# A linear attention feeding two gated layers on one core: another program order of the opening, and a subtraction moved from GpSimd to VectorE inside the weight decoding

## The chip, the core and the metric

The kernel runs on one NeuronCore of a Trainium2 chip. Its engines run side by side, each through its own queue in order: TensorE (PE, matrix products; PEld are its weight loads), VectorE (DVE), ScalarE (ACT), GpSimd (POOL), and SyncE (SP), which here issues every DMA. The metric is the device time of one execution in microseconds, lower is better.

## The reference

```
# r,k,v: (4 batches, 8 heads, 768 tokens, 48)
for t in range(S):
    cur = (u*k_t) outer v_t
    y_t = r_t @ (state + cur)
    state = w*state + k_t outer v_t
x  = y as (3072 tokens, 384)
h  = x @ w_in                                # 384 -> 2048
x  = (h * clip(h+3, 0, 6) / 6) @ w_out       # 2048 -> 384
out = (sigmoid(x @ w_gate) * (x @ w_val)) @ w_out2   # 384 -> 1536 -> 384
```

All inputs and the output are float32.

## The kernel before

**Attention.** 24 chunks of 128 tokens (chunk c is batch c mod 4, sequence part c div 4). `load_chunk` fetches a chunk twice: `rk` (r and k transposed, 448 KB) and `vkr` (natural order, 576 KB). `prep` scales them on VectorE, or on GpSimd for r·k and k from chunk 8 on, and makes on ScalarE the eight diagonal tiles of `aeo`. `stage_A` forms k·r products on TensorE, which VectorE then copies under a mask into `aeo` (L297, L298). `stage_Y` computes y, ScalarE copies it to `ysb` (L355, L358), and four DMAs per chunk lay it out as `xf`, features by tokens. `stage_U` updates the state `Z`. `split_chunk` turns `xf` into a rounded part `xhi` (ScalarE, L370) and the rest `xlo` (VectorE, L371), so that three fast products give a float32 one.

**Weights.** 34 pairs of weight tiles come as 64-bit words (`raw`, 768 KB each). Decoding a pair is a pipeline of three slots (`slot`): ScalarE reads the words (L78, L79), VectorE joins them in four operations (L85, L87, L89, L91), then ScalarE makes the rounded half (L135) and VectorE the rest (`w`, L123). A call of `slot` does one of these steps for each of three pairs. `fetch_next` issues the loads.

**Feed-forward.** Stage one works on six blocks of 512 tokens (four chunks each), each in 16 steps f: nine products `h`, then on ScalarE t (L559), on VectorE t (L560), `gh` on ScalarE (L393) and `gl`, the rest t - gh, on VectorE or GpSimd (L394). Two steps later nine products `o` follow (`out1`). `steps1` is the order of the steps: the first LEAD steps of block 0 alone, then block 1 and block 0 in turn. Step numbers i count in that order. The products of a step's first half of tokens (`halves`) are issued ahead for i = 0 and 1. A psum buffer of `h` is one of two, so the products of step i wait for t of step i-2. Stage two has six blocks of 12 steps: nine products `h` (gate), nine `pv`, sigmoid, t (L646), `gh`, `gl` on GpSimd, and twelve products `o` two steps later.

**What sets the order.** Up to step i = LEAD+2 a scheduler places the instructions of each engine from the program's order and its own estimate of times; from i = LEAD+3 on the program's order holds (`manual_schedule`). `due` gives the steps at which the attention stages of later blocks run. The last block of stage one calls `slot` in every odd step, stage two in every step while pairs are left. At the end, `values_load` brings a flag into a register of every engine, and a branch skips a fallback loop.

**Buffers that matter here.** `wpool` has 17 buffers for `raw`, `w` and, for the first four chunks, `vkr` and `aeo`. `ysb` has one buffer, `xf` three, `rk` three.

Of the kernel before, what the change touches and what calls it, by code (L numbers as in the profile page):

```python
# [63 lines left out]
def decay_attention_ffn_ffn(ctx, tc, rkT, vkr, wT, uN, uT, flip_d, ident_d, mask_d, wst, out):  # L64
# [13 lines left out]
        nc.scalar.activation(a.bitcast(F32), raw[:, :, 1].bitcast(F32), AF.Abs)  # L78
        nc.scalar.activation(r, raw[:, :, 0], AF.Copy, scale=2.0 ** -29)  # L79

    def join_words(*tiles):

        for a, r, raw in tiles:
            af = a.bitcast(F32)
            nc.vector.tensor_scalar(out=af, in0=af, scalar1=TOP, scalar2=BOTTOM, op0=ALU.min, op1=ALU.max)  # L85
        for a, r, raw in tiles:
            nc.vector.tensor_scalar(out=a, in0=a, scalar1=3, scalar2=0x3FFFFFF8, op0=ALU.logical_shift_left, op1=ALU.bitwise_and)  # L87
        for a, r, raw in tiles:
            nc.vector.scalar_tensor_tensor(out=a, in0=raw[:, :, 1], scalar=0xC0000000, in1=a, op0=ALU.bitwise_and, op1=ALU.bitwise_or)  # L89
        for a, r, raw in tiles:  # L90
            nc.vector.tensor_tensor(out=a, in0=a, in1=r, op=ALU.add)  # L91
# [32 lines left out]
        for x, (kind, f) in enumerate(PAIRS[i]):  # L124
            parts[kind][f] = w[:, :, x * DM:(x + 1) * DM]

    def slot(early=None, n_early=0):

        old, mid = pipe
        new = None  # L130
        if old:
            i, a, raw = old
            pool = early if NP1 <= i < NP1 + n_early else wpool
            w = pool.tile([P, 2, 2 * DM], F32R, tag="w", name="w")
            nc.scalar.activation(w[:, 0, :], a.bitcast(F32), AF.Copy)  # L135
        if count["begun"] < count["fetched"]:
            k = count["begun"]
            raw = raws.pop(k)
            b = dec_p.tile([P, 2 * DM], U32, tag="a", name="a")
            read_words(b, raw[:, :, 0], raw)  # L140
            new = k, b, raw
            count["begun"] += 1
        if mid:
            join_words((mid[1], mid[2][:, :, 0], mid[2]))
        if old:
            finish((i, a, w))
        pipe[:] = mid, new
# [109 lines left out]
    def prep(c, part):  # L257

        if c >= n_chunks:
            return  # L260
        if part == 0:
            t, n = loads.pop(c)
            v, k, r = n[:, 0], n[:, 1], n[:, 2]
            for p in ((0, 2), (2, 4)) if c == 0 else ((0, 4),):
                tp = t[:, :, p[0]:p[1]]
                nc.vector.tensor_tensor(out=tp, in0=tp, in1=wb[:, :, p[0]:p[1]], op=ALU.mult)
            side = nc.vector if c < 2 * B else nc.gpsimd
            side.tensor_tensor(out=r, in0=r, in1=k, op=ALU.mult)  # L268
            side.tensor_tensor(out=r, in0=r, in1=uB, op=ALU.mult)
            prepped[c] = {"R": t[:, 0], "K": t[:, 1], "v": v, "k": k, "r": r}  # L270
            return
        q = prepped[c]
        if part == 1:
            q["c"] = a2.tile([C, H], F32, tag="cd", name="cd")
            nc.vector.tensor_reduce(out=q["c"], in_=q["r"], axis=mybir.AxisListType.X, op=ALU.add)  # L275
        elif part == 2:
            pool, tag = (wpool, "w") if c < B else (a2, "aeo")
            ab = pool.tile([C, 2, NP, C], F32, tag=tag, name="aeo")
            for i, nm in enumerate(("ae", "ao")):
                q[nm] = ab[:, i]  # L280
                cs = q["c"].rearrange("p (n x) -> p n x", x=2)[:, :, i:i + 1]
                for p in range(NP):
                    nc.scalar.activation(q[nm][:, p, :], flip, AF.Copy, scale=cs[:, p, :])  # L283
        elif c // B < NCH - 1:
            side = nc.vector if c < 2 * B else nc.gpsimd
            side.tensor_tensor(out=q["k"], in0=q["k"], in1=WN, op=ALU.mult)
# [41 lines left out]
    def stage_Y(c):  # L328
        q = prepped[c]
        n, b = c // B, c % B  # L330
        pool, tag = (ps_o, "o") if c < B else (ps_h, "h") if c in BETWEEN else (ps_a, "A")
        ps = [pool.tile([P, NP, C], F32, tag=tag, name="y") for _ in range(1 if n == 0 else 2)]

        def place(x, p):

            y = p % 2
            m = D if y else 64
            return ps[x if n > 0 else 0][64 * y:64 * y + m, 2 * x + p // 2, :], m

# [12 lines left out]
        def after():
            ysb = a1.tile([ROWS, NP, C], F32, tag="ysb", name="ysb")
            if n == 0:
                nc.scalar.activation(ysb, ps[0][0:ROWS], AF.Copy)  # L355
            else:
                for x in range(2):
                    nc.scalar.activation(ysb[:, 2 * x:2 * x + 2, :], ps[x][0:ROWS, 2 * x:2 * x + 2, :], AF.Copy)  # L358
            x = xf[c] = xf_p.tile([P, KC, C], F32, tag="xf", name="xf")
            for kc, (r0, nr, q0) in ((0, (0, 32, 0)), (1, (32, 16, 0)), (1, (64, 16, 16)), (2, (80, 32, 0))):  # L360
                nc.sync.dma_start(out=x[4 * q0:4 * (q0 + nr), kc, :], in_=ysb[r0:r0 + nr])
        return after
# [25 lines left out]
        return ps  # L388

    def split_g(g, n, side):  # L390
        gh = g_p.tile([P, 512], F32R, tag="gh", name="gh")
        gl = g_p.tile([P, 512], F32R, tag="gl", name="gl")
        nc.scalar.activation(gh[:, :n], g[:, :n], AF.Copy)  # L393
        side.tensor_tensor(out=gl[:, :n], in0=g[:, :n], in1=gh[:, :n].bitcast(F32), op=ALU.subtract)  # L394
        return gh, gl

    three = const.tile([P, 1], F32, name="three")
# [1 line left out]

    LEAD = 6
    steps1 = [(0, f) for f in range(LEAD)]
    for f in range(F1):
        steps1 += [(1, f)] + [(0, f + LEAD)] * (f + LEAD < F1)
# [34 lines left out]
    due = []  # L440
    for j in range(1, len(BLOCKS1)):
        these = [x for x in stages if x[2] == j]
        first, span = (1, LEAD - 1) if j == 1 else (LEAD + 2, 2 * F1 - 2 - LEAD - 2) if j == 2 else (F1 * (j - 1), F1)
        due += [first + span * k // len(these) for k in range(len(these))]

    nxt = 0
# [10 lines left out]
    load_chunk(1)  # L457
    load_chunk(2)
    load_chunk(3)
    fetch1(4)  # L460
    powers()
    on_a, on_y = {}, {}
    for c in range(B):
        for part in range(3):
            prep(c, part)
        on_a[c] = stage_A(c)
        if c == 0:
            wtab = powers_ahead()
        if c == 1:
            power_transposes(wtab)  # L470
        if c > 0:
            on_a[c - 1]()
            on_y[c - 1] = stage_Y(c - 1)
            slot()
        if c > 1:
            on_y[c - 2]()
            fetch1(3 + c)
    on_a[B - 1]()
    on_y[B - 1] = stage_Y(B - 1)
    slot()  # L480
# [15 lines left out]
    split_chunk(3)  # L496
    slot()
    prep(3, 3)
    load_chunk(B)
    fetch1(6)  # L500
    load_chunk(B + 1)

    st1 = starts(BLOCKS1)
    outs = {}
# [46 lines left out]
    last = F1 * (len(BLOCKS1) - 1)  # L551
    pending = []
    for i, (j, f) in enumerate(steps1):
        if i == LEAD + 3:
            ctx.enter_context(tc.manual_schedule())
        n = BLOCKS1[j]
        ps = proj_into(halves[i], win[f], xs[j], n, HALF) if i < 2 else proj(win[f], xs[j], n)
        t = t_p.tile([P, 512], F32, tag="t", name="t")
        nc.scalar.activation(t[:, :n], ps[:, :n], AF.Relu, bias=three)  # L559
        nc.vector.scalar_tensor_tensor(out=t[:, :n], in0=t[:, :n], scalar=6.0, in1=ps[:, :n], op0=ALU.min, op1=ALU.mult)  # L560
        gs[i] = split_g(t, n, nc.vector if i < 2 * F1 else nc.gpsimd)
        pending.append(i)
        if i == 0:
            after_u = stage_U(2)
# [39 lines left out]
            fetch_next(3, w2pool)  # L604
        if i >= last:
            next_x1(0, f)
            if f % 2 == 1:
                slot(w2pool, EARLY)
                fetch_next(1, w2pool)


    steps2 = [(j, f) for j in range(len(BLOCKS2)) for f in range(F2)]
# [25 lines left out]
    for i, (j, f) in enumerate(steps2):  # L638
        n = BLOCKS2[j]
        x = xs[("2", j)]  # L640
        pg = proj(wga[f], x, n)
        pv = ps_a.tile([P, 512], F32, tag="A", name="pv")
        proj_into(pv, wva[f], x, n)
        t = t_p.tile([P, 512], F32, tag="t", name="t")
        nc.scalar.activation(t[:, :n], pg[:, :n], AF.Sigmoid)  # L645
        nc.vector.tensor_tensor(out=t[:, :n], in0=t[:, :n], in1=pv[:, :n], op=ALU.mult)  # L646
        gs[i] = split_g(t, n, nc.gpsimd)
        if f >= LAG:
            out2(i - LAG)
        slot(w2pool, EARLY)  # L650
        fetch_next(1, w2pool)
        if j + 1 < len(BLOCKS2):
            next_x1(j + 1, f)
        if f == F2 - 1:
            for k in range(LAG):
                out2(i - LAG + 1 + k)
# [2 lines left out]


    T = 32
    bad = nc.values_load(outside, min_val=0, max_val=1)
    with tc.If(bad > 0):
        x0 = tc.dram_tile([DM, NT], F32, name="x0")
        with ExitStack() as fb:
# [168 lines left out]
```

## Time and profile before

| | |
|---|---|
| median of 3 runs | 1000.77 us (999.6 to 1002.5) |
| the profiled execution | 1000.27 us, its span 998.5 us |
| PE busy | 953.9 us, 96% |
| PEld busy | 800.0 us, 80% |
| DVE busy | 437.4 us, 44% |
| ACT busy | 397.6 us, 40% |
| POOL busy | 240.2 us, 24% |
| mean granted clock of TensorE | 0.981 of 2.4 GHz |

A profile is one execution. Busy shares are means over stages with different limits, so the tables by stretch below say more. The DMA share is the mean over 16 DMA engines. Of the 24 chunks' attention, the loads and the decoding, most lies beside the products; what is outside them is at the start, at the change from stage one to stage two, and at the end.

### The profile page before, as it was taken

To read this page: it belongs to the slowest core of one execution; us is meant where nothing else is said; L and a number is where in the kernel's file an instruction comes from. 1 tells how busy PE (TensorE), PEld (TensorE's weight loads), DVE (VectorE), ACT (ScalarE), POOL (GpSimd) and SP (SyncE) were. 2 spreads that over 40 slices of the span, in tenths; PEclk is the share of its full clock that TensorE was granted. 3 is DMA by queue.
4 is the path that set the end of the run, shared out by engine and by line. 5 is a ranking of instruction groups with operands and counts; after the bars stand their busy time and mean duration, and the time that the engine had idled before them with its cause. 6 is when DMAs were issued, how large, how long until landed. Compare 5 with 4: busy or idle time off the path is not lost.

```text
span 998.5 us, 13269 instructions
## 1 busy us (share of the span) xinstructions
PE 953.9 (96%) x5320; PEld 800.0 (80%) x5320; DVE 437.4 (44%) x645; ACT 397.6 (40%) x754; POOL 240.2 (24%) x188
## 2 busy tenths in 40 slices
PE   5589799999999999999999999999999999999997
PEld 4477587788888888787887887888888888888886
DVE  7999587544344434323576995122122122122111
ACT  3857274444444444443556663222222222222211
POOL 0003201103444543432332221221221221221221
PEclk9679999999999999999999999999999999999999
DMA  9754241131312222100612441001001001000001
GB/s 304 216 195 164 77 142 30 52 106 43 90 52 82 63 89 82 51 17 23 238 64 71 168 142 43 22 1 55 9 1 55 9 1 56 9 1 32 1 1 35
DMA packets 38582, 72.10 MB, mean 72 GB/s; under 512 B 4208, under 2 KB 26096, under 8 KB 38512
## 3 DMA queue, kind: packets, MB, share of 16 engines
q1 hardware_dynamic: 38512, 71.17, 22.7%
q8 instruction: 43, 0.70, 0.3%
q14 instruction: 27, 0.22, 0.1%
HBM read 57.00 MB, written 9.44 MB: 67 GB/s over the span
## 4 chain that ended last, share of the span: by engine, by line
PE 83%; DMA 5%; DVE 5%; ACT 2%; issue 2%; POOL 1%; SPq 0%; POOLq 0%; ACTq 0%; DVEq 0%
PE o L110 32%; PE h L110 31%; PE pv L110 15%; DMA vkr<-in_vkr 3%; PE y L110 3%; PE A L110 2%; DMA xf<-ysb 1%; POOL gl L394 1%; DVE w L123 1%; DVE t L560 1%; ACT aeo L283 1%; PE U L110 1%; DVE a L91 1%; DVE a L89 1%; ACT gh L393 1%
## 5 line engine op out<-in xcount | busy, mean ns | idle before, releaser
L110 PE MATMUL h<-xhi,w 128*128 128x512 f32 (+1 forms) x1020 | 343.6, 393 | 4.3 <-DVE t L560 2.8
L394 POOL TENSOR_TENSOR gl<-t,gh 128x512 fp32r<-128x512 f32 x136 | 178.5, 1312 | 567.0 <-ACT gh L393 561.4
L110 PEld LDWEIGHTS h<-xhi,w 128*128 128x128 f32 x1020 | 193.1, 190 | 46.0 <-DVE t L560 4.0
L393 ACT ACTIVATE gh<-t 128x512 fp32r<-128x512 f32 x168 | 106.1, 632 | 238.9 <-DVE t L646 156.0
L110 PE MATMUL h<-xlo,w 128*128 128x512 f32 (+1 forms) x510 | 199.8, 392 | 1.4 <-DVE xlo L371 1.3
L110 PE MATMUL o<-gh,w 128*128 128x512 f32 x576 | 195.0, 396 | 0.0
L646 DVE TENSOR_TENSOR t<-t,pv 128x512 f32<-128x512 f32 x72 | 49.5, 687 | 267.8 <-PE pv L110 266.9
L110 PE MATMUL o<-w,gh 128*128 128x384 f32 x576 | 147.5, 336 | 1.1 <-DVE w L123 1.0
L110 PE MATMUL pv<-xhi,w 128*128 128x512 f32 x432 | 144.8, 389 | 1.1 <-DVE w L123 1.1
L560 DVE SCALAR_TENSOR_TENSOR t<-t,h 128x512 f32<-128x512 f32 x96 | 65.7, 686 | 179.8 <-ACT t L559 179.8
L110 PEld LDWEIGHTS o<-gh,w 128*128 128x128 f32 x576 | 108.4, 188 | 24.9 <-issue 0.9
L559 ACT ACTIVATE t<-h,three 128x512 f32<-128x512 f32 x96 | 65.5, 685 | 132.5 <-PE h L110 130.7
L110 PE MATMUL o<-gl,w 128*128 128x512 f32 x288 | 113.5, 394 | 3.2 <-DVE gl L394 2.4
L110 PEld LDWEIGHTS h<-xlo,w 128*128 128x128 f32 x510 | 96.8, 190 | 19.6 <-DVE xlo L371 1.9
L110 PEld LDWEIGHTS o<-w,gh 128*128 128x128 f32 x576 | 105.6, 188 | 6.4 <-DVE w L123 1.3
L110 PE MATMUL o<-w,gl 128*128 128x384 f32 x288 | 97.0, 337 | 0.0
L110 PEld LDWEIGHTS pv<-xhi,w 128*128 128x128 f32 x432 | 81.1, 188 | 18.6 <-DVE w L123 1.5
L645 ACT ACTIVATE t<-h 128x512 f32<-128x512 f32 x72 | 42.9, 596 | 131.3 <-PE h L110 131.2
L110 PE MATMUL pv<-xlo,w 128*128 128x512 f32 x216 | 84.0, 389 | 0.0
L268 POOL TENSOR_TENSOR vkr<-vkr 128x384 f32<-128x384 f32 x16 | 30.1, 1882 | 179.4 <-DMA vkr<-in_vkr 179.4
L110 PEld LDWEIGHTS o<-gl,w 128*128 128x128 f32 x288 | 54.5, 189 | 14.7 <-DVE gl L394 2.8
L283 ACT ACTIVATE aeo<-flip,cd 128x128 f32<-128x128 f32 x192 | 58.7, 392 | 6.6 <-DVE cd L275 6.6
(68 smaller groups left out, 805.5 us busy)
## 6 DMA issues: line engine op xcount, KB each, us to landing
raw<-in_weights SPq DMA_DIRECT2D x34, 768.0 KB, 5.7
vkr<-in_vkr SPq DMA_DIRECT2D x24, 576.0 KB, 5.0
rk<-in_rkT SPq DMA_DIRECT2D x24, 448.0 KB, 4.3
x<-ob SPq DMA_DIRECT2D x18, 256.0 KB, 2.1
x2f<-x SPq DMA_DIRECT2D x24, 192.0 KB, 3.0
out<-ob SPq DMA_DIRECT2D x24, 192.0 KB, 1.9
xf<-ysb SPq DMA_DIRECT2D x48, 64.0 KB, 2.1
xf<-ysb SPq DMA_DIRECT2D x48, 32.0 KB, 2.0
```

Source lines behind the costliest of these rows:

```text
L89: nc.vector.scalar_tensor_tensor(out=a, in0=raw[:, :, 1], scalar=0xC0000000, in1=a, op0=ALU.bitwise_and, op1=ALU.bitwise_or)
L91: nc.vector.tensor_tensor(out=a, in0=a, in1=r, op=ALU.add)
L110: nc.tensor.matmul(o, l, r, start=start, stop=stop, skip_group_check=True)
L123: nc.vector.tensor_tensor(out=w[:, 1, :], in0=a.bitcast(F32), in1=w[:, 0, :].bitcast(F32), op=ALU.subtract)
L268: side.tensor_tensor(out=r, in0=r, in1=k, op=ALU.mult)
L283: nc.scalar.activation(q[nm][:, p, :], flip, AF.Copy, scale=cs[:, p, :])
L393: nc.scalar.activation(gh[:, :n], g[:, :n], AF.Copy)
L394: side.tensor_tensor(out=gl[:, :n], in0=g[:, :n], in1=gh[:, :n].bitcast(F32), op=ALU.subtract)
L559: nc.scalar.activation(t[:, :n], ps[:, :n], AF.Relu, bias=three)
L560: nc.vector.scalar_tensor_tensor(out=t[:, :n], in0=t[:, :n], scalar=6.0, in1=ps[:, :n], op0=ALU.min, op1=ALU.mult)
L645: nc.scalar.activation(t[:, :n], pg[:, :n], AF.Sigmoid)
L646: nc.vector.tensor_tensor(out=t[:, :n], in0=t[:, :n], in1=pv[:, :n], op=ALU.mult)
```

## The change

- **Opening.** Before the loop over the first four chunks, one pair of weights is fetched instead of four. The loop is written out, with the decode slots and fetches at other places: two slots after chunk 0's y, one after chunk 2's, and so on. The scheduler makes another order of it.
- **`ysb`** of chunks 0 to 3 comes out of `wpool`, so that each has a buffer of its own.
- **LEAD** is 5 instead of 6: block 1 begins one step earlier. The scheduler's part now ends at i = 11 (LEAD+7), and the stages of block 2 begin at step LEAD+4.
- **`gl` in decode steps.** In the odd steps of stage one's last block, and in stage two while pairs are left in the pipeline, `gl` runs on VectorE between the second and third joining operation. The call of `slot` moves into `split_g`, ahead of `out1`/`out2` and `next_x1`. These are 20 of the 136 `gl` on GpSimd.
- **`values_load`** moves from the end to step 6 of the last block.

```
-    def join_words(*tiles):
+    def join_words(*tiles, between=lambda: None):
...
             nc.vector.tensor_scalar(out=a, in0=a, scalar1=3, scalar2=0x3FFFFFF8, ...)
+        between()
...
         def after():
-            ysb = a1.tile([ROWS, NP, C], F32, tag="ysb", name="ysb")
+            pool, tag = (wpool, "w") if c < 4 else (a1, "ysb")
+            ysb = pool.tile([ROWS, NP, C], F32, tag=tag, name="ysb")
...
     def split_g(g, n, side):
...
-        side.tensor_tensor(out=gl[:, :n], in0=g[:, :n], in1=gh[:, :n].bitcast(F32), op=ALU.subtract)
+        def rest(engine):
+            engine.tensor_tensor(out=gl[:, :n], in0=g[:, :n], in1=gh[:, :n].bitcast(F32), op=ALU.subtract)
+        if side is slot:
+            slot(w2pool, EARLY, lambda: rest(nc.vector))
+            fetch_next(1, w2pool)
+        else:
+            rest(side)
...
-    LEAD = 6
+    LEAD = 5
...
-        first, span = ... (LEAD + 2, 2 * F1 - 2 - LEAD - 2) if j == 2 else ...
+        first, span = ... (LEAD + 4, 2 * F1 - 2 - LEAD - 2) if j == 2 else ...
...
-    fetch1(4)
+    fetch1(1)
     powers()
-    for c in range(B):
-        for part in range(3):
-            prep(c, part)
-        on_a[c] = stage_A(c)
...
+    for part in range(3):
+        prep(0, part)
+    on_a[0] = stage_A(0)
+    wtab = powers_ahead()
+    for part in range(3):
+        prep(1, part)
+    on_a[1] = stage_A(1)
+    power_transposes(wtab)
+    on_a[0]()
+    on_y[0] = stage_Y(0)
+    slot()
+    slot()
+    for part in range(3):
+        prep(2, part)
+    on_a[2] = stage_A(2)
+    on_a[1]()
+    on_y[1] = stage_Y(1)
+    fetch1(5)
+    on_y[0]()
...
-        if i == LEAD + 3:
+        if i == LEAD + 7:
             ctx.enter_context(tc.manual_schedule())
...
-        gs[i] = split_g(t, n, nc.vector if i < 2 * F1 else nc.gpsimd)
+        gs[i] = split_g(t, n, nc.vector if i < 2 * F1 else slot if i >= last and f % 2 == 1 else nc.gpsimd)
...
-        gs[i] = split_g(t, n, nc.gpsimd)
+        gs[i] = split_g(t, n, slot if pipe != [None, None] else nc.gpsimd)
...
+        elif f == F2 // 2:
+            bad = nc.values_load(outside, min_val=0, max_val=1)
...
-    bad = nc.values_load(outside, min_val=0, max_val=1)
```

Line numbers below are those of the kernel in question; L90, L92, L124, L401, L375, L585 after are L89, L91, L123, L394, L371, L560 before.

**First place: VectorE, ahead of the first t of block 1.** `t_1016` before and `t_978` after are t of (block 1, f = 0); `xlo_679` and `xlo_676` are the last chunk of block 1's x; `w_…` is a decoded pair. Before:

```order
L91 ISA a_910<-raw_808,a_910 128x1536
L323 SCALAR_TENSOR_TENSOR Z3_124<-Z3_124,W128_119,U_975 112x48 x4
L394 TENSOR_TENSOR gl_934<-t_930,gh_933 128x512
L89 SCALAR_TENSOR_TENSOR a_996<-raw_918,a_996 128x768
L123 TENSOR_TENSOR w_1058<-a_910,w_1058 128x768
L91 ISA a_996<-raw_918,a_996 128x1536
L371 TENSOR_TENSOR xlo_679<-xf_967,xhi_678 128x3x128
L560 SCALAR_TENSOR_TENSOR t_1016<-t_1016,h_1006 128x512
L560 SCALAR_TENSOR_TENSOR t_1042<-t_1042,h_1032 128x512
```

After, on the same engine:

```order
L92 ISA a_734<-raw_627,a_734 128x1536
L124 TENSOR_TENSOR w_842<-a_619,w_842 128x768
L375 TENSOR_TENSOR xlo_676<-xf_929,xhi_675 128x3x128
L401 TENSOR_TENSOR gl_868<-t_864,gh_867 128x512
L90 SCALAR_TENSOR_TENSOR a_844<-raw_742,a_844 128x768
L124 TENSOR_TENSOR w_956<-a_734,w_956 128x768
L85 TENSOR_SCALAR a_958<-a_958 128x768
L92 ISA a_844<-raw_742,a_844 128x1536
L87 TENSOR_SCALAR a_958<-a_958 128x768
L585 SCALAR_TENSOR_TENSOR t_978<-t_978,h_968 128x512
L585 SCALAR_TENSOR_TENSOR t_1004<-t_1004,h_994 128x512
```

Before, ten pairs are decoded by `t_1016` (`w_1058` is the tenth); after, eight by `t_978` (`w_956` is the eighth).

**Second place: SP's queue of DMAs, from chunk 2's loads to the first `xf`.** `rk_145` is chunk 3, `rk_465` / `rk_455` chunk 4; `vkr_467` to `vkr_569` (after: 457 to 562) are chunks 4 to 6. Before:

```order
L173 DMA vkr_147<-in_vkr 128x1152
L154 DMA raw_149<-in_weights 128x1536
L154 DMA raw_151<-in_weights 128x1536
L154 DMA raw_153<-in_weights 128x1536
L154 DMA raw_155<-in_weights 128x1536
L173 DMA vkr_467<-in_vkr 128x1152
L173 DMA vkr_471<-in_vkr 128x1152
L173 DMA vkr_569<-in_vkr 128x1152
L170 DMA rk_145<-in_rkT 112x1024
L170 DMA rk_465<-in_rkT 112x1024
L154 DMA raw_300<-in_weights 128x1536
L170 DMA rk_469<-in_rkT 112x1024
```

After:

```order
L176 DMA vkr_147<-in_vkr 128x1152
L157 DMA raw_149<-in_weights 128x1536
L176 DMA vkr_457<-in_vkr 128x1152
L176 DMA vkr_461<-in_vkr 128x1152
L176 DMA vkr_562<-in_vkr 128x1152
L173 DMA rk_145<-in_rkT 112x1024
L173 DMA rk_455<-in_rkT 112x1024
L157 DMA raw_284<-in_weights 128x1536
L157 DMA raw_286<-in_weights 128x1536
L157 DMA raw_288<-in_weights 128x1536
L157 DMA raw_290<-in_weights 128x1536
L173 DMA rk_459<-in_rkT 112x1024
```

The same twelve loads stand ahead of the first `xf` DMA, four of the weights behind the chunk loads instead of ahead of them. After the first chunk's four `xf` DMAs follow, before, `raw_354` and the next chunk's `xf`; after, `rk_560`, `raw_340` and then the next chunk's `xf`.

**Third place: VectorE in a decode step of stage two.** Before:

```order
L646 TENSOR_TENSOR t<-t,pv 128x512
L85 TENSOR_SCALAR a<-a 128x768
L87 TENSOR_SCALAR a<-a 128x768
L89 SCALAR_TENSOR_TENSOR a<-raw,a 128x768
L91 ISA a<-raw,a 128x1536
L123 TENSOR_TENSOR w<-a,w 128x768
```

After:

```order
L668 TENSOR_TENSOR t<-t,pv 128x512
L85 TENSOR_SCALAR a<-a 128x768
L87 TENSOR_SCALAR a<-a 128x768
L401 TENSOR_TENSOR gl<-t,gh 128x512
L90 SCALAR_TENSOR_TENSOR a<-raw,a 128x768
L92 ISA a<-raw,a 128x1536
L124 TENSOR_TENSOR w<-a,w 128x768
```

One instruction is added to VectorE's step, and one of GpSimd's goes.

## Rows read from the trace of the kernel before

**Rows 1.** Stretches: from:to length, busy PE PEld DVE ACT POOL, clock, DMA share, GB/s.

```profile
0.00:200.00 200.00, 166.44 (x1112) 131.79 (x1113) 154.98 (x259) 110.78 (x231) 23.26 (x23) 0.91 0.47 147
200.00:500.00 300.00, 299.95 (x1881) 242.56 (x1881) 118.89 (x190) 134.01 (x278) 108.75 (x83) 1.00 0.26 78
500.00:620.00 120.00, 115.61 (x536) 98.02 (x535) 95.17 (x111) 67.15 (x100) 30.83 (x22) 1.00 0.28 93
620.00:985.00 365.00, 365.00 (x1759) 321.14 (x1757) 66.53 (x83) 84.06 (x144) 76.08 (x59) 1.00 0.06 20
```

**Rows 2.** The same view, two stretches of the opening.

```profile
28.00:65.80 37.80, 23.10 (x212) 18.86 (x213) 35.35 (x57) 25.63 (x60) 0.00 (x0) 0.68 0.64 172
65.80:112.08 46.28, 42.36 (x253) 32.50 (x253) 39.51 (x67) 28.41 (x56) 15.29 (x9) 0.89 0.55 184
```

**Rows 3.** The chain that ended last, opening: start, length, what.

```profile
32.15 9.40 DMA xf<-ysb
...
65.80 2.16 PE y L110 x15
67.96 2.00 PE A L110 x8
69.96 3.38 PE h L110 x9
...
74.03 2.05 PE h L110 x9
```

**Rows 4.** VectorE's instructions in order of time, opening: start, length, what.

```profile
65.64 1.27 DVE L560 SCALAR_TENSOR_TENSOR t<-t,h 128x512 f32<-128x512 f32 x2
...
90.13 0.95 DVE L91 CUSTOM_DVE_ANT_0 a<-raw,a 128x1536 uint16<-128x1536 uint16 x1
...
92.79 1.22 DVE L266 TENSOR_TENSOR rk<-rk,W 112x1024 f32<-112x1024 f32 x1
93.93 0.74 DVE L298 COPY_PREDICATED aeo<-mask,A 128x512 f32<-128x512 uint32 x1
94.55 0.68 DVE L394 TENSOR_TENSOR gl<-t,gh 128x512 fp32r<-128x512 f32 x1
95.14 0.56 DVE L85 TENSOR_SCALAR a<-a 128x768 f32<-128x768 f32 x1
95.61 0.95 DVE L89 SCALAR_TENSOR_TENSOR a<-raw,a 128x768 uint32<-128x768 uint32 x1
96.48 0.95 DVE L123 TENSOR_TENSOR w<-a,w 128x768 fp32r<-128x768 f32 x1
97.35 0.55 DVE L371 TENSOR_TENSOR xlo<-xf,xhi 128x384 fp32r<-128x384 f32 x1
...
105.97 0.55 DVE L371 TENSOR_TENSOR xlo<-xf,xhi 128x384 fp32r<-128x384 f32 x1
```

**Rows 5.** TensorE's waits in order of time; in brackets idle before, releaser.

```profile
103.50 0.80 PE L110 MATMUL o<-gl,w 128*128 128x512 f32 x1 [2.42 <-DVE gl L394]
112.08 0.50 PE L110 MATMUL h<-xhi,w 128*128 128x512 f32 x1 [1.50 <-DVE t L560]
...
527.62 0.50 PE L110 MATMUL h<-xhi,w 128*128 128x512 f32 x1 [1.34 <-DVE t L560]
537.12 0.50 PE L110 MATMUL o<-gl,w 128*128 128x512 f32 x1 [0.79 <-POOL gl L394]
...
609.09 0.73 PE L110 MATMUL pv<-xhi,w 128*128 128x512 f32 x2 [1.11 <-DVE w L123]
614.66 0.45 PE L110 MATMUL o<-w,gh 128*128 128x384 f32 x1 [1.01 <-DVE w L123]
```

**Rows 6.** One `gl` on GpSimd and the join beside it, order of time.

```profile
520.47 1.48 POOL L394 TENSOR_TENSOR gl<-t,gh 128x512 fp32r<-128x512 f32 x1 [0.68 <-ACT gh L393]
...
520.85 1.92 DVE L89 SCALAR_TENSOR_TENSOR a<-raw,a 128x768 uint32<-128x768 uint32 x1
```

**Rows 7.** The instructions of line L662: duration ns, starts.

```profile
L662 SPq TENSOR_LOAD <-outside x1: 563/563/563, 992.9 to 992.9; - x1
```

More of the change, by code (lines that the diff above doesn't have):

```diff
@@ L125, in finish, with slot @@
             parts[kind][f] = w[:, :, x * DM:(x + 1) * DM]
-    def slot(early=None, n_early=0):
+    def slot(early=None, n_early=0, between=lambda: None):
         old, mid = pipe
@@ L143, in slot @@
         if mid:
-            join_words((mid[1], mid[2][:, :, 0], mid[2]))
+            join_words((mid[1], mid[2][:, :, 0], mid[2]), between=between)
+        else:
+            between()
         if old:
@@ L266, in prep @@
                 nc.vector.tensor_tensor(out=tp, in0=tp, in1=wb[:, :, p[0]:p[1]], op=ALU.mult)
-            side = nc.vector if c < 2 * B else nc.gpsimd
+            side = nc.vector if c < 2 * B and c not in () else nc.gpsimd
             side.tensor_tensor(out=r, in0=r, in1=k, op=ALU.mult)
@@ L393, in split_g @@
         nc.scalar.activation(gh[:, :n], g[:, :n], AF.Copy)
-        side.tensor_tensor(out=gl[:, :n], in0=g[:, :n], in1=gh[:, :n].bitcast(F32), op=ALU.subtract)
+        def rest(engine):
[3 more added lines that the diff above has]
+            fetch_next(1, w2pool)
+        else:
+            rest(side)
         return gh, gl
@@ L442, in decay_attention_ffn_ffn @@
         these = [x for x in stages if x[2] == j]
-        first, span = (1, LEAD - 1) if j == 1 else (LEAD + 2, 2 * F1 - 2 - LEAD - 2) if j == 2 else (F1 * (j - 1), F1)
+        first, span = (1, LEAD - 1) if j == 1 else (LEAD + 4, 2 * F1 - 2 - LEAD - 2) if j == 2 else (F1 * (j - 1), F1)
         due += [first + span * k // len(these) for k in range(len(these))]
@@ L459, in decay_attention_ffn_ffn @@
     load_chunk(3)
-    fetch1(4)
+    fetch1(1)
     powers()
     on_a, on_y = {}, {}
-    for c in range(B):
-        for part in range(3):
-            prep(c, part)
-        on_a[c] = stage_A(c)
[L467 to L477, printed above, removed]
+    for part in range(3):
[17 more added lines that the diff above has]
+    on_y[0]()
+    for part in range(3):
+        prep(3, part)
+    on_a[3] = stage_A(3)
+    on_a[2]()
+    on_y[2] = stage_Y(2)
+    slot()
+    fetch1(6)
+    on_y[1]()
     on_a[B - 1]()
@@ L498, in decay_attention_ffn_ffn @@
     prep(3, 3)
-    load_chunk(B)
+    load_chunk(4)
     fetch1(6)
-    load_chunk(B + 1)
+    load_chunk(5)
     st1 = starts(BLOCKS1)
@@ L606, in decay_attention_ffn_ffn @@
             next_x1(0, f)
-            if f % 2 == 1:
-                slot(w2pool, EARLY)
-                fetch_next(1, w2pool)
     steps2 = [(j, f) for j in range(len(BLOCKS2)) for f in range(F2)]
@@ L646, in decay_attention_ffn_ffn @@
         nc.vector.tensor_tensor(out=t[:, :n], in0=t[:, :n], in1=pv[:, :n], op=ALU.mult)
-        gs[i] = split_g(t, n, nc.gpsimd)
+        gs[i] = split_g(t, n, slot if pipe != [None, None] else nc.gpsimd)
         if f >= LAG:
             out2(i - LAG)
-        slot(w2pool, EARLY)
-        fetch_next(1, w2pool)
         if j + 1 < len(BLOCKS2):
             next_x1(j + 1, f)
+        elif f == F2 // 2:
+            bad = nc.values_load(outside, min_val=0, max_val=1)
         if f == F2 - 1:
```

## The prediction

> **What bounds the kernel now.** I read the busy time by stretch first [rows 1]. TensorE is busy all of 620 to 985 us and 299.95 of the 300 us before 500, at full clock. It loses 33.6 us of the first 200 and 4.4 us between 500 and 620. So only three places can give time: the opening, the change from stage one to stage two, and the tail.
>
> Then the opening in two stretches [rows 2]. From 28.0 to 65.8 us TensorE works 23.1 of 37.8 us at a mean clock of 0.68, and VectorE 35.35 of 37.8: VectorE is the bound. The chain says how this ends [rows 3]: `y`, `A`, and the first full `h` (step i = 2) at 69.96. The releaser is on VectorE: it forms the first t of block 0 at 65.64 [rows 4], and the products of step 2 need the psum buffer that this t frees. From 65.8 to 112.08 TensorE is busy for 42.36 of 46.28 us. Its two waits there, 2.42 and 1.50 us, are both for VectorE, the second for t of the first step of block 1 [rows 5]. That step needed the last chunk of block 1's x, whose `xlo` VectorE reached at 105.97 [rows 4].
>
> Last the waits of the later places [rows 5]: 1.34, 0.79, 1.11 and 1.01 us, all for VectorE's decoding, its t, or a `gl`.
>
> **The change part by part.**
>
> *The opening.* I price it by the rows in VectorE's queue. Pitches, start to start [rows 4]: `rk` 1.14, `gl` 0.59, L85 0.47, L89 0.87, L123 0.87. L91 lasts as long as L89 (0.95) and counts 0.87; L87 and the 128x384 operations last as L85 and count 0.47; t counts as `gl`.
>
> First point, t of step 0. Up to it the new order has two L123, one L89 and one L91 fewer (4 x 0.87 = 3.48) and three 128x384 operations more (1.41). So t begins 2.1 earlier, at 63.6, if VectorE waits as much as now, and is done at 64.2. Now `y` of chunk 5 and half of `A` of chunk 6 come between this t and step 2's products, 2.16 + 2.00 us at a low clock [rows 3]. In the new order their inputs are ready earlier and they stand ahead, so step 2 can start near 64.2 instead of 69.96.
>
> Second point, t of the first step of block 1. Counted in the order up to it, six of L89, L91 and L123 go (5.22), one L85 and one L87 (0.94), one t and one `gl` (1.18), and one `rk` is added (1.14): net 6.2. These are decodes put off, eight pairs before it instead of ten, and one step less of block 0. Now VectorE could have begun this t at 105.97 + 0.47 = 106.44; after, at 100.2, done at 100.9.
>
> TensorE goes on from there with step 7, where it now goes on with step 8 at 112.08. It has one step less behind it: nine `h` and nine `o`, 2 x 2.05 [rows 3] = 4.1. Gain: 112.08 - 100.9 - 4.1 = 7.1 us.
>
> Could TensorE itself be later than 100.9? Its work from step 2 to that point now takes 112.08 - 69.96 = 42.1; less 3.9 of waits, 4.1 of the missing step and 1.0 for the half of `A` already done, 33.1. From 64.2 this ends at 97.3. VectorE remains the bound, by 3.6 us. That gives the better end: were VectorE never late, 112.08 - 97.3 - 4.1 = 10.7. For the worse end, VectorE's waits double: it stands idle for 2.45 us in the first stretch and 6.77 in the second [rows 2], about 4.8 of these behind 106.5 where it no longer sets anything. The other 4.4 again would leave 2.7. I take 7.1, since both orders put the same operations on the same engine.
>
> What is late next: the put-off decodes. VectorE owes two pairs, 7.1 us, right after 100.9. From then on a pair is wanted every second step, some 8.2 us of products. `gl` of the new step is due at about 104 in VectorE's queue; TensorE has two times nine `h` (4.1 us) until 105. So I add nothing.
>
> *Edits taken at nothing.* A buffer of its own for each early `ysb` lets chunks 1 to 3 be copied without waiting for the last `xf`; its worth is inside the sums above, since VectorE's queue is full. The later stages of block 2 and three more steps under the scheduler lie where TensorE now waits for nothing (200 to 500, [rows 1]). `slot` ahead of `next_x1` puts `xhi` behind ScalarE's wait for the join; that `xhi` is for the next block, a step's products hide it.
>
> *`gl` on VectorE in decode steps.* Beside a `gl` on GpSimd (1.48 us) the third joining operation takes 1.92 us instead of 0.95 [rows 6, 4]. With `gl` on VectorE, 0.97 goes and 0.59 is added: VectorE's step is 0.38 shorter. All four late waits hang on such a step, so 4 x 0.38 = 1.5 us. Ends: all four go, 4.25; or L89 does not shorten and each step is 0.59 longer, -2.4.
>
> *The flag.* SP's register load takes 0.56 us after the last DMA issue, ahead of the branch [rows 7]; it goes. In the midst of the products it costs nothing if TensorE's queue runs ahead, 0.5 if not. I take 0.6, bounds 0.1 and 0.6.
>
> *Sum.* 7.1 + 1.5 + 0.6 = 9.2 us. The profiled execution took 1000.27 (span 998.5 and 1.77 around it): 991.1. The median of the runs is 0.5 above it, so 991.5.
>
> **The rivals.**
>
> *The first x is no earlier.* The first `xf` is issued at 32.15 and lands 9.40 later [rows 3]. The same 6 `rk`, 7 `vkr` and 5 `raw` (10.6 MB) stand ahead of it in both orders, so it need not land sooner, and chunk 1's now has `rk` and `raw` (1.2 MB) ahead of it, 7 us at the 172 GB/s of the stretch [rows 2]. Then step 0's t keeps its time, 2.1 of the gain goes, and the time is 993.5. Against it: VectorE's queue reaches the first `xlo` some 3 us later than now. The Trainium skill, DMA: Bandwidth & Descriptors, section Queues, rings and completion order, says that each DMA engine takes descriptors in ring order; by that rule the first `xf` waits for all 10.6 MB, and the trace's 9.40 us agrees.
>
> *Step 5 waits for chunk 7.* With LEAD 5 block 1 begins one step earlier. If chunk 7's x hangs on its loads, `y` and transport rather than on VectorE's queue, its `xlo` stays near 105.97; t is done at 107.1, and the gain is 112.08 - 107.1 - 4.1 = 0.9, with the rest 3.0: 997.5. For it: `xf` and `vkr` share SP's queue with the put-off weights. Against it: those weights' loads stand behind chunk 7's in the new order.
>
> *The clock.* The new opening spreads TensorE's work from 64.2 to 100.9. At full clock it is 33.1 less the 4.7 that the mean 0.89 costs on 42.36 busy us [rows 2]: 28.4, a busy share of 77%. Now 61% went with a clock of 0.68 and 92% with 0.89. If the clock stays at its lower level (1.2 GHz) for all of it, 56.8 us end at 121: 20 us lost, net 11 slower, 1002 to 1011. It decides for slower by 3 when 20.5 of the 28.4 us run at the lower level. At 0.79, the mean of the two stretches, the work ends at 100.2 and costs nothing. The Trainium skill, TensorE: Matmul & The Clock Gate, section HAM oscillation, says that pauses between groups of products let the clock fall, so that the next group starts at the lower level; by it this rival would hold if VectorE fed TensorE in pieces. The low clock after idle time in the first stretch agrees.
>
> *VectorE is not late at all*: 10.7 + 1.5 + 0.6, 988.
>
> **How the numbers follow.** Forecast 0.54, the better case 0.12, the first x no earlier 0.15, chunk 7 0.13, the clock 0.06. The forecast's own ends: 10.7 + 4.25 + 0.6 gives 985, 2.7 - 2.4 + 0.1 gives 1000. The range runs from 985 to 999, which leaves out the clock and the last of the worse end. What can be told from no change here is about 0.3%, 3 us. Faster by more: the first three and a little of chunk 7, 0.83; same: the rest of it and a corner of the worse end, 0.10; slower: the clock and what I do not see, 0.07.
>
> **What would show it.** In the new profile the first full `h` starts near 64 and t of block 1's first step ends near 101; `xlo` of chunk 7 is done near 95 to 97, since thirteen instructions of decoding, one t and two `gl` fewer and one `rk` more stand ahead of it (10.3 us). The wait of 2.42 for `gl` is gone. The join beside `gl` takes 0.95, and the four late waits shrink by about 0.4 each. Behind the last product about 0.6 us less. It is wrong if step 2 starts after 68, if `xlo` of chunk 7 comes after 102 or waits for a DMA, if the clock from 64 to 101 is below 0.75, or if VectorE's put-off decodes make TensorE wait for `w` or `gl` after 105.

## The result, and the profile after

The changed kernel takes 987.61 us in the median of 4 runs (985.62 to 987.79), against 1000.92 us for the kernel before (4 runs beside it): a ratio over all these runs of 0.9862 with a 95% interval of 0.9843 to 0.9881. The profiled execution took 987.73 us with a span of 985.8, so 12.5 us less than the profiled one before. Forecast were 991.5 us and a gain of 9.2.

To find where the time went I use two landmarks of TensorE that both kernels have: the last unbroken row of 27 products `h` in stage one, and the last row of 36 products `o`. The chain shows them in either kernel (start, length, what). First the kernel before:

```profile
473.06 6.12 PE h L110 x27
...
985.62 6.28 PE o L110 x36
```

Then the changed kernel:

```profile
464.27 6.12 PE h L111 x27
...
972.92 6.28 PE o L111 x36
```

Up to the first landmark the changed kernel is 8.79 us ahead (opening), between the two it gains 512.56 - 508.65 = 3.91 (change of stage), and behind the second nothing: 12.7, the difference of the spans. Forecast for the three places were 7.1, 1.5 and 0.6.

The stretches of the changed kernel that answer to [rows 1] and [rows 2]:

```profile
0.00:200.00 200.00, 174.41 (x1151) 139.68 (x1152) 157.50 (x265) 115.08 (x237) 27.76 (x23) 0.92 0.47 147
200.00:500.00 300.00, 299.95 (x1882) 242.56 (x1881) 122.32 (x196) 137.33 (x281) 107.45 (x82) 1.00 0.26 81
500.00:620.00 120.00, 118.68 (x555) 101.71 (x554) 85.17 (x122) 65.88 (x97) 6.46 (x5) 1.00 0.30 97
...
28.00:64.00 36.00, 29.41 (x248) 24.85 (x249) 33.30 (x54) 25.54 (x57) 0.00 (x0) 0.62 0.69 203
64.00:100.00 36.00, 31.11 (x208) 23.73 (x206) 34.72 (x57) 25.99 (x54) 18.09 (x8) 0.95 0.74 253
```

TensorE is busy 8 us more of the first 200 and 3 us more between 500 and 620, where GpSimd's work falls from 30.83 to 6.46 us. The instructions on which the opening's sum stood, VectorE first (answers to [rows 4]):

```profile
63.60 0.68 DVE L585 SCALAR_TENSOR_TENSOR t<-t,h 128x512 f32<-128x512 f32 x1
...
94.03 0.55 DVE L375 TENSOR_TENSOR xlo<-xf,xhi 128x384 fp32r<-128x384 f32 x1
...
100.06 1.28 DVE L585 SCALAR_TENSOR_TENSOR t<-t,h 128x512 f32<-128x512 f32 x2 [1.34 <-ACT t L584]
```

and TensorE, with its waits in brackets (answers to [rows 5]):

```profile
64.62 0.50 PE L111 MATMUL h<-xhi,w 128*128 128x512 f32 x1
...
92.66 0.73 PE L111 MATMUL h<-xhi,w 128*128 128x512 f32 x2 [3.19 <-ACT xhi L374]
...
100.80 0.50 PE L111 MATMUL h<-xhi,w 128*128 128x512 f32 x1
...
150.08 0.66 PE L111 MATMUL y<-rk,Z 48*48 48x128 f32 x14 [0.51 <-DVE t L585]
...
596.85 0.72 PE L111 MATMUL pv<-xhi,w 128*128 128x512 f32 x2 [0.61 <-DVE w L124]
600.98 0.44 PE L111 MATMUL o<-w,gh 128*128 128x384 f32 x1 [0.16 <-ACT w L136]
601.98 0.44 PE L111 MATMUL o<-w,gh 128*128 128x384 f32 x1 [0.55 <-DVE w L124]
```

t of step 0, the first full `h` and the step after the first of block 1 stand where the prediction put them (63.6, 64.2, 100.9). But block 1's first step waits 3.19 us for chunk 7's `xhi`, and VectorE then sits idle 1.34 us: VectorE's queue is not what this t waits for. Of the four late waits two are gone whole and two are shorter: 4.25 us have become 1.32 (0.61 for `pv`, 0.16 and 0.55 for `o`).

### The profile page after: what moved, and what is told of

It reads as the page before. It is cut to its first block, busy times and chain, and to the rows that moved or that the text cites. A ratio compares the mean times of both kernels' runs of the same rounds, so it can differ in the third digit from the quotient of the medians.

```text
span 985.8 us, 13258 instructions
## 1 busy us (share of the span) xinstructions
PE 952.2 (97%) x5320; PEld 800.8 (81%) x5320; DVE 431.3 (44%) x665; ACT 399.9 (41%) x754; POOL 216.5 (22%) x168
## 4 chain that ended last, share of the span: by engine, by line
PE 88%; DMA 5%; DVE 5%; ACT 1%; issue 1%; SPq 0%; DVEq 0%; ACTq 0%
PE o L111 34%; PE h L111 34%; PE pv L111 15%; DMA raw<-in_weights 4%; PE y L111 3%; PE A L111 2%; PE U L111 1%; DVE w L124 1%; DMA uB<-in_uN 1%; DVE a L90 1%; DVE a L92 1%; DVE t L585 1%; DMA rk<-in_rkT 0%; DVE rk L269 0%; DMA xf<-ysb 0%
## 5 line engine op out<-in xcount | busy, mean ns | idle before, releaser
L401 POOL TENSOR_TENSOR gl<-t,gh 128x512 fp32r<-128x512 f32 x116 | 150.2, 1295 | 583.4 <-ACT gh L398 583.4
L585 DVE SCALAR_TENSOR_TENSOR t<-t,h 128x512 f32<-128x512 f32 x96 | 65.7, 686 | 178.7 <-ACT t L584 178.7
```

What stands on the lines that cost most here:

```text
L401: engine.tensor_tensor(out=gl[:, :n], in0=g[:, :n], in1=gh[:, :n].bitcast(F32), op=ALU.subtract)
```

## Experiments

Each is read at the landmarks: the start of the 27 `h` (473.06 before, 464.27 after) for the opening, and the distance to the last 36 `o` (512.56 and 508.65) for the change of stage. The second repeats within 0.06 us wherever the late code is the same. The first is less sharp: executions of the same opening scatter by 3.7 us (last section), so an opening is judged by the medians as well. Ratios are to the kernel before, run in the same session, with a 95% interval.

### The late part undone

```diff
-        gs[i] = split_g(t, n, slot if pipe != [None, None] else nc.gpsimd)
+        gs[i] = split_g(t, n, nc.gpsimd)
         if f >= LAG:
             out2(i - LAG)
+        slot(w2pool, EARLY)
+        fetch_next(1, w2pool)
```

(and the same in the last block of stage one.)

> The changed kernel with the late part undone: gl of the decode steps on GpSimd again, and the decode call behind the products as before. Theory A (the two parts add, and the late part is worth all that lies between 472 and 618 us of the trace of before, 3.9): the third joining operation takes 1.92 us again beside gl, the waits of 1.34, 0.79, 1.11 and 1.01 us come back, and the profiled execution takes 987.7 + 3.9 = 991.6. Theory B (the prediction's term, 0.38 for each of four waits, and the rest of the gain belongs to the opening): 987.7 + 1.5 = 989.2.

Ratio 0.9894 (0.9873 to 0.9914); distance 512.56, exactly that of the kernel before; the waits are back. The two halves add, and the late part is worth 3.91, not 1.5.

### Engine and place apart

The late part is two edits: `gl` moves to VectorE, and the decode call moves ahead of the `o` products. First the engine alone undone:

```diff
-            slot(w2pool, EARLY, lambda: rest(nc.vector))
+            rest(nc.gpsimd)
+            slot(w2pool, EARLY)
```

> Late part, engine alone undone: gl of the decode steps on GpSimd again, the decode call stays at its new place, ahead of the o products. Read from the start of the 27 products h near 463 us to that of the last 36 products o: 512.56 us in the kernel before and in the run with both undone, 508.65 in the changed kernel. Theory A (the engine counts, since the joining operation beside GpSimd's gl takes 1.92 instead of 0.95): 511 to 512.6. Theory B (the place counts, since the join is queued earlier): 508.6 to 509.5.

Distance 510.34, ratio 0.9882 (0.9854 to 0.9910). The wait of 1.34 for t stays away, 0.79 becomes 0.33, and the two for `w` are 1.11 and 1.01 as before. So the place is worth 512.56 - 510.34 = 2.22, and the engine, at the new place, the other 1.69. Neither theory holds alone.

What the place changes is on VectorE. In the kernel before `next_x1` stands ahead of the join, and so does its `xlo`:

```profile
501.17 0.69 DVE L560 SCALAR_TENSOR_TENSOR t<-t,h 128x512 f32<-128x512 f32 x1 [1.27 <-ACT t L559]
502.97 1.34 DVE L371 TENSOR_TENSOR xlo<-x2f,xhi 128x384 fp32r<-128x384 f32 x1 [1.11 <-ACT xhi L370]
504.24 0.55 DVE L85 TENSOR_SCALAR a<-a 128x768 f32<-128x768 f32 x1
```

At the new place, `gl` still on GpSimd:

```profile
493.74 0.69 DVE L586 SCALAR_TENSOR_TENSOR t<-t,h 128x512 f32<-128x512 f32 x1 [1.51 <-ACT t L585]
494.34 0.55 DVE L85 TENSOR_SCALAR a<-a 128x768 f32<-128x768 f32 x1
...
499.24 0.55 DVE L375 TENSOR_TENSOR xlo<-x2f,xhi 128x384 fp32r<-128x384 f32 x1
```

Before, VectorE waits 1.11 us for `xhi` and spends 1.34 on `xlo`, and the join begins 3.07 us behind the start of t; at the new place it begins 0.60 behind it, and `xlo` comes afterwards, without a wait and in 0.55. The kernel before loses this in four steps of the last block (`xlo` at 485.88, 494.03, 502.97 and 511.90). Then the place alone undone, with `gl` ahead of the whole join:

```diff
-gs[i] = split_g(t, n, slot if pipe != [None, None] else nc.gpsimd)
+gs[i] = split_g(t, n, nc.vector if pipe != [None, None] else nc.gpsimd)
 ...
+        slot(w2pool, EARLY)
```

> Late part, place alone undone: gl of the decode steps on VectorE, ahead of the whole join and not within it, and the decode call behind the o products as before. Read as in the run with gl on GpSimd. Theory A (engine): 508.6 to 509.5, and the joining operation takes 0.95 throughout. Theory B (place): 511 to 512.6.

Distance 515.24, ratio 0.9928 (0.9903 to 0.9953): worse than the kernel before by 2.68. VectorE in one such step:

```profile
590.50 0.68 DVE L671 TENSOR_TENSOR t<-t,pv 128x512 f32<-128x512 f32 x1
591.88 0.69 DVE L401 TENSOR_TENSOR gl<-t,gh 128x512 fp32r<-128x512 f32 x1 [0.70 <-ACT gh L398]
592.49 0.55 DVE L85 TENSOR_SCALAR a<-a 128x768 f32<-128x768 f32 x1
593.08 0.56 DVE L87 TENSOR_SCALAR a<-a 128x768 uint32<-128x768 uint32 x1
593.67 0.96 DVE L90 SCALAR_TENSOR_TENSOR a<-raw,a 128x768 uint32<-128x768 uint32 x1
```

and in the changed kernel:

```profile
591.71 0.69 DVE L668 TENSOR_TENSOR t<-t,pv 128x512 f32<-128x512 f32 x1 [0.68 <-PE pv L111]
592.31 0.55 DVE L85 TENSOR_SCALAR a<-a 128x768 f32<-128x768 f32 x1
592.90 0.56 DVE L87 TENSOR_SCALAR a<-a 128x768 uint32<-128x768 uint32 x1
593.37 0.69 DVE L401 TENSOR_TENSOR gl<-t,gh 128x512 fp32r<-128x512 f32 x1
593.98 0.95 DVE L90 SCALAR_TENSOR_TENSOR a<-raw,a 128x768 uint32<-128x768 uint32 x1
```

The joining operation takes 0.95 in both, as forecast. But `gl` needs ScalarE's `gh`, and ahead of the join it holds VectorE idle for 0.70 in each of the 20 steps; within the join two operations fill that wait (it is left in two of the 20, which have no join). So what the engine gains depends on the place. (The Trainium skill, SBUF — State Buffer, section Who interferes with whom, says that a VectorE operation with two SBUF inputs contends with a GpSimd operation that reads SBUF, and that the port pair they share is an exclusive lock; 1.92 beside `gl` on GpSimd [rows 6] and 0.95 without it agree.)

### The flag

```diff
-        elif f == F2 // 2:
-            bad = nc.values_load(outside, min_val=0, max_val=1)
 ...
+    bad = nc.values_load(outside, min_val=0, max_val=1)
     with tc.If(bad > 0):
```

> The changed kernel with the flag's register load behind the last DMA issue again. Theory A (the branch's end is set by the landing of the last output and by what every engine does at the branch, not by the load): same time, 987.7 within 0.2, and 6.6 us from the end of the last product to the end of the span. Theory B (the prediction's term): 0.6 more, 988.3, and 7.2 us behind the last product.

Ratio 0.9873 (0.9850 to 0.9896), 6.77 us from the end of the last product to the end of the span, or 7.11 from its start, which is how the rest is read. That is between the theories (6.6 and 7.2 from the end), so the load was multiplied:

```diff
+    for _ in range(3):
+        nc.values_load(outside, min_val=0, max_val=1)
     bad = nc.values_load(outside, min_val=0, max_val=1)
```

> The changed kernel with the flag loaded four times behind the last DMA issue instead of once in the midst. One load with its register operations takes SP 0.77 us (0.54 + 0.19 + 0.04). Read from the start of the last product to the end of the span: 6.96, 7.11 and 7.53 in three kernels with one load at the end, 6.94, 6.95 and 6.44 in three without. Theory A (the load is on the path that ends the program, as the prediction has it): 7.2 + 3 x 0.77 = 9.5. Theory B (the landing of the last output and the code behind the branch set the end, the load lies beside them): at most 8.

8.50, ratio 0.9901 (0.9873 to 0.9929), between the theories again: three more loads cost 1.3 against the mean of 7.20 below, 0.43 each, so the load is on the path with somewhat more than half of its 0.77. Over all traces of this study the stretch is 6.96, 7.00, 7.11, 7.39 and 7.53 with one load at the end (mean 7.20), and 6.42, 6.44, 6.49, 6.53, 6.63, 6.74, 6.94 and 6.95 without (mean 6.64). The flag is worth 0.56 on the mean. The two groups overlap, four of the five with the load are of the older kernel, and the one pair of traces of before and after (6.96, 6.94) happens not to show it.

### The opening's parts

It has three: one `ysb` buffer per early chunk, LEAD 5 with its two numbers, and the order of loads and first decodes. LEAD 6 in the new kernel:

```diff
-    LEAD = 5
+    LEAD = 6
 ...
-        first, span = ... (LEAD + 4, 2 * F1 - 2 - LEAD - 2) if j == 2 else ...
+        first, span = ... (LEAD + 2, 2 * F1 - 2 - LEAD - 2) if j == 2 else ...
 ...
-        if i == LEAD + 7:
+        if i == LEAD + 3:
```

> The changed kernel with block 1 begun at step 6 again, and with it the first stages of block 2 and the written order where they were; the new order of loads, decodes and ysb buffers stays. Theory A (the opening's gain is VectorE's and the transport's order, not the number of steps): TensorE fills its wait of 3.19 for chunk 7's x with the sixth step; t of block 1's first step comes 2.3 to 3.6 us later than 100.06, with one step (4.1 us) less behind it, so 0.5 to 1.8 faster: 986 to 987.2. Theory B (beginning block 1 a step earlier is what gains): the step comes back, 987.7 + 4.1 = 991.8.

27 `h` at 467.19, median 991.93, ratio 0.9909 (0.9883 to 0.9934): theory B. The sixth step doesn't fill the gap, since its decodes stand ahead of its own `gl` on VectorE:

```profile
94.87 0.80 PE L111 MATMUL o<-gl,w 128*128 128x512 f32 x1 [4.12 <-DVE gl L401]
106.22 0.50 PE L111 MATMUL h<-xhi,w 128*128 128x512 f32 x1 [1.50 <-DVE t L585]
118.89 0.66 PE L111 MATMUL y<-rk,Z 48*48 48x128 f32 x14 [1.20 <-DVE t L585]
```

LEAD 5 in the old one (the same edit the other way):

> The kernel before with only LEAD 5 and the two numbers that go with it (first stages of block 2, start of the written order); loads, decodes, ysb and gl as before. Theory A (VectorE's order gains): VectorE reaches t of block 1's first step 2.6 us later than before by the pitches of its rows (more decoding stands ahead of it), and one step more (4.1) lies behind it: slower by 3 to 6.7, 1003 to 1007. Theory B (the step count gains): faster, 1000.3 - 7 = 993.

474.77, ratio 0.9997 (0.9984 to 1.0010): no gain, and less loss than theory A. The count of VectorE's queue does not hold there, since in the kernel before VectorE waited 4.82 us ahead of that t, so its queue was not the bound:

```profile
111.33 1.28 DVE L560 SCALAR_TENSOR_TENSOR t<-t,h 128x512 f32<-128x512 f32 x2 [4.82 <-ACT t L559]
```

One buffer for `ysb` in the new kernel:

```diff
-            pool, tag = (wpool, "w") if c < 4 else (a1, "ysb")
-            ysb = pool.tile([ROWS, NP, C], F32, tag=tag, name="ysb")
+            ysb = a1.tile([ROWS, NP, C], F32, tag="ysb", name="ysb")
```

> The changed kernel with one ysb buffer for the first four chunks, as before. Read at the start of the 27 products h near 463 us (464.27 in the changed kernel, 463.0 to 463.2 in two other executions with the same opening). Theory A (the prediction's term: VectorE's queue is full, so the copies may wait): 463 to 464.3, no change. Theory B (the first x come late again, ScalarE's xhi of chunks 1 to 3 at 47.3, 52.1 and 57.1 as before, and the order that is made from it puts decodes ahead of t: by the pitches of its rows VectorE comes to t of step 0 2.2 and to t of block 1's first step 2.7 us later): 465.5 to 467.

471.28, ratio 0.9945 (0.9927 to 0.9963): worse than theory B. The scheduler made another order of VectorE's queue here, from about 50 us on, so this run, like each of the others on the opening, prices an edit together with the order that comes of it, not the wait for a buffer alone. TensorE's waits:

```profile
57.69 0.80 PE L111 MATMUL h<-xhi,w 128*128 128x256 f32 x2 [3.67 <-ACT xhi L373]
...
97.78 1.22 PE L111 MATMUL h<-xhi,w 128*128 128x512 f32 x2 [2.64 <-ACT xhi L373]
107.83 0.50 PE L111 MATMUL h<-xhi,w 128*128 128x512 f32 x1 [1.50 <-DVE t L584]
```

The same buffers alone in the old kernel:

> The kernel before with only the ysb buffers of the first four chunks (as in the change). Read at the start of the 27 products h near 473 us: 473.06 in the kernel before, 463.0 to 466.7 in six executions of the changed opening, 471.3 there with one ysb. Theory A (ysb is worth about 7 us by itself): 466. Theory B (it pays only in the new order: by the pitches of its rows VectorE reaches t of block 1's first step at the same place as before, 85.4 us into its queue in both): 472 to 474.

472.31, ratio 0.9984 (0.9970 to 0.9999): theory B. Buffers and LEAD 5 together there:

> The kernel before with the ysb buffers and LEAD 5 with its two numbers; loads, first decodes and gl as before. Theory A (these two make the gain, the order of loads and first decodes nothing): 463 to 467 at the 27 products h. Theory B (VectorE's queue: t of block 1's first step stands at 84.1 in it, against 79.2 with the new order): 4.9 later than the changed opening, 468 to 471.

469.86, ratio 0.9949 (0.9932 to 0.9966): theory B. Chunk 7's `xhi` lets TensorE start at 93.36, nearly as in the changed kernel, but t of block 1's first step ends later by its place on VectorE, and the next step starts at 104.75 instead of 100.80: 3.95, forecast 4.9. Last the order alone (the edits of one `ysb` and of LEAD 6 in one kernel):

> The changed kernel with one ysb and with LEAD 6 and its two numbers: of the opening only the order of loads and first decodes is new. Theory A (by VectorE's queue t of block 1's first step stands at 85.4, as in the kernel before): 472 to 474 at the 27 products h, no gain. Theory B (the order is worth the 5.9 by which the run with LEAD 6 and all ysb buffers was ahead of the kernel before): 467.

481.69 in the profiled execution, the longest of ten (994.25 to 1004.68), in which the granted clock stayed near 0.50 from 58 to 78 us; ratio 0.9962 (0.9941 to 0.9982). By the medians, in the table below, theory A: no gain. To put all on one scale I take the differences of the medians to the kernel before, and add 4.5 (3.91 + 0.56) where the late part and the flag are in:

| in the opening | 27 `h` against 473.06 | by the medians |
|---|---|---|
| `ysb` | -0.8 | -1.0 |
| LEAD 5 | +1.7 | +0.7 |
| order | +8.6 | +1.5 |
| `ysb`, LEAD 5 | -3.2 | -4.2 |
| order, LEAD 5 | -1.8 | -2.3 |
| order, `ysb` | -5.9 | -5.2 |
| all three | -8.8 | -8.8 |

By the medians the parts alone sum to +1.2; together they give -8.8. By the intervals of the ratios each figure is uncertain by 1.3 to 2.6 us and the sum of three by about 3, so the difference of 10 is clear, while the signs of the single parts hardly are.

### A version with two more moves

```diff
-        if i == LEAD + 7:
+        if i == LEAD + 5:
 ...
+        def ahead():
+            between()
+            if old and early and i >= NP1 + 4:
+                finish((i, a, w))
```

(`ahead` then goes into the join as `between`, and the later `finish` is left out for these pairs.)

> The changed kernel with two things more: the written order begins two steps earlier (step 10), which takes one rk product from ahead of t of block 1's first step on VectorE; and in decode steps from the seventeenth pair on the last subtraction of the older pair comes ahead of the third joining operation instead of behind the fourth. Opening, theory A (VectorE sets it): t of block 1's first step 1.1 earlier, 97.7 at full clock, the 27 products h at 462 to 465.6. Theory B (chunk 7's transport sets it): 463 to 466.7, no change. Late stretch, to the last 36 products o (508.65 in the changed kernel): theory A (w is late by its place in VectorE's queue): the wait of 0.61 goes, and 0.27 of draining and refilling with it, 507.8; theory B (ScalarE's copy or the raw words are late): 508.65.

Distance 507.75: the wait of 0.61 is gone, theory A, 0.9 us. The opening gave nothing (468.30, later than either theory; it is one of the late executions of the last section), and the wait of 1.20 ahead of `y` came back at 124.58. Ratio 0.9876 (0.9856 to 0.9897): not better than the change as it is.

## Why the prediction was right, and where it was not

*Opening, 7.1 forecast, 8.8 measured.* From 112.08 to 100.80 with one step less done are 11.28 - 4.1 = 7.2. The rest is a wait I had not counted: in the kernel before TensorE stops for 1.20 us ahead of `y` at 124.71, and the changed kernel does not. It goes with the step at which the written order begins. It is there in all five kernels in which the scheduler's part ends at i = 8 or 9: before, the three others with LEAD 6, and the version with two more moves, which has LEAD 5 and block 2 at LEAD + 4 like the changed kernel. Where the scheduler works up to i = 11 it is gone, also in the old kernel with LEAD 5: there products `o` stand ahead of `y` (at 119.88 and 122.02 in the changed kernel), in the five `y` comes straight behind products `h`. With draining and refilling (below) the wait costs 1.47. "The later stages of block 2 and three more steps under the scheduler lie where TensorE now waits for nothing" was wrong: I read that from a window that begins at 200.

*"VectorE remains the bound, by 3.6 us"* fails in its last stretch. The chain that ended last in the changed kernel runs along VectorE's queue to chunk 7's `aeo`, and from there through the transport:

```profile
82.49 0.74 DVE aeo L300
...
83.27 2.42 PE y L111 x28
...
88.04 3.94 DMA xf<-ysb
...
92.08 0.53 ACT xhi L374
...
92.66 3.79 PE h L111 x10
```

So TensorE stood still until 92.66 behind `y`, four DMAs and ScalarE, 9.4 us that the count of VectorE's queue left out: the way of the rival on chunk 7, only 12 us earlier than that rival feared (`xlo` at 94.03 against 105.97), because `aeo` itself came early. The sign "waits for a DMA" came true of this `xhi` (1.91 us). That the number came out is in part luck. The sum set TensorE's restart before, 112.08, against the earliest time of t in VectorE's new queue; but before, VectorE stood idle for 4.82 us ahead of that t, so the 6.2 by which its queue became shorter were not what TensorE had waited for. And in the new order queue and transport nearly tie: in the execution with the flag at the end the same t began at 98.79 without a wait of VectorE's. "Its worth is inside the sums, since VectorE's queue is full" named the wrong reason for `ysb`: without it, and with the order that comes of that, chunk 7's x comes 5 us later and 7.0 of 8.8 are lost (6.5 by the medians).

*`gl` on VectorE, 1.5 forecast, 3.9 measured.* The price of the engine came out (1.69 at the new place; 0.50, 0.30 and 0.33 off three waits, and draining and refilling). The step that failed is "`slot` ahead of `next_x1`", taken at nothing: the place is worth 2.22. The prediction looked at ScalarE's `xhi` alone; what counts is that VectorE's `xlo` no longer holds up the join by some 2.5 us in a step. By 527.62 that delay had reached TensorE: ScalarE's t of this step (526.18) stood behind its part of the decoding, which had waited 3.46 us for the join. No run moves `slot` ahead of `out1` and `next_x1` one at a time, so this cause is read from the traces.

*The flag, 0.6 forecast:* 0.56 on the mean of thirteen traces, 0.02 in this pair.

*The rivals.* The first x came no earlier (`xhi` of chunk 0 at 42.83, before at 42.50), as the first rival said; yet t of step 0 lost nothing by it, since chunks 1 to 3 came 0.2 to 2.8 us earlier through their buffers (47.09, 49.77 and 54.34; with one `ysb` 47.79, 52.54 and 57.12). The clock's mean was 0.95 from 64 to 100, so that rival did not come.

## What to carry to other kernels

Where two chains meet at one point (here x's transport and VectorE's queue ahead of block 1's first t), an edit to either alone is worth about nothing, and one undone takes 3 to 7 of the 8.8 us: price such edits together, and test them in all pairs. Before moving an operation to another engine, look at what it waits for there and put it behind work that fills the wait. The distance of two landmarks between which TensorE's work is the same repeats here to 0.06 us, where the times themselves scatter by 2 us and more; a landmark behind an opening that scatters does not have that sharpness.

## What the runs showed of the hardware

The opening's time is not the same in each execution of the same instructions: in six executions of the changed opening, with VectorE's operations in the same order, the 27 `h` begin at 463.02, 463.16, 463.74, 464.27, 466.40 and 466.72. The granted clock goes with it. Two stretches of the changed kernel:

```profile
50.00:58.00 8.00, 8.00 (x46) 7.09 (x42) 6.22 (x12) 5.93 (x15) 0.00 (x0) 0.62 0.84 247
58.00:66.00 8.00, 8.00 (x84) 6.85 (x83) 8.00 (x18) 4.70 (x9) 0.00 (x0) 1.00 0.39 119
```

and of the execution that began them at 466.40 (`gl` on GpSimd at the new place, the same opening):

```profile
50.00:58.00 8.00, 8.00 (x39) 7.22 (x39) 6.48 (x13) 6.14 (x15) 0.00 (x0) 0.50 0.83 241
58.00:66.00 8.00, 8.00 (x59) 6.91 (x60) 6.38 (x12) 1.51 (x4) 0.00 (x0) 0.56 0.09 37
```

TensorE had the same idle time before (6.58 and 6.37 us busy of the 10 before 50) and is busy without a break in both, but the clock rises to its upper level (2.4 GHz) at about 56 us in the first and 65 in the second, by these means, and t of step 0 comes at 65.35 instead of 63.60. The other late executions (466.72, and the version with two more moves at 468.30) have 0.50 and 0.53 to 0.57 in these two stretches. So the clock rival was about the right thing at the wrong place: the rise of the clock is worth some 3 us between executions. The record of the clock can fail: in the run with `gl` ahead of the whole join (463.74) it reads 1.00 all the way, though the products of 128x256 start 0.21 us apart until 56 us, as in the others, and 0.12 apart from 60 us on. There I go by the starts.

The clock also fell behind the wait for chunk 7 in four of the six executions: after waits of 2.19, 2.25, 2.27 and 3.19 us products of 128x512 start up to 0.43 us apart for some three us, after waits of 2.32 and 2.39 they stay at 0.23. From 90 to 98 us the granted clock was 0.79 in the changed kernel (3.19) and 1.00 with the flag at the end (2.32). The Trainium skill, TensorE: Matmul & The Clock Gate, section HAM oscillation, says that pauses between groups of products let the clock fall; here it fell after four of six such pauses, and not by their length. The fall cost almost nothing: from the first product behind the wait to the step after block 1's first are 8.14 to 8.26 us where it fell, and 8.12 and 8.14 where it did not, since there TensorE waited 1.28 us for VectorE's t instead.

A wait of TensorE's costs more than the idle time shown. Starts of 128x512 products lie 0.227 us apart; around the wait of 0.61 in the changed kernel they read

```profile
595.85 0.39 PE L111 MATMUL pv<-xlo,w 128*128 128x512 f32 x1
596.85 0.72 PE L111 MATMUL pv<-xhi,w 128*128 128x512 f32 x2 [0.61 <-DVE w L124]
597.41 0.40 PE L111 MATMUL pv<-xlo,w 128*128 128x512 f32 x1
```

that is 0.77 late in the second line and 0.11 more in the third: 0.27 beside the 0.61, which I call draining and refilling of the engine. Read in the same way, the four late waits of before cost 5.4, not 4.25.

GpSimd may be held off by VectorE as well: one elementwise product of 128x384 there, between 1.0 and 2.0 us elsewhere beyond 110 us, took 8.21 us from 91.38 on, while VectorE went from operation to operation without a pause until 98.72. In the five other executions of this opening one such operation took 8.69 to 8.71. That VectorE caused it is not shown by a run of its own.
